# Fourier-convolution and gated-unit kernel: the loads of the second Fourier stage move from SyncE's queue to GpSimd's

## The chip, the cores and the metric

The kernel runs on one core of one Trainium2 chip. A core has five engines that run side by side: TensorE (PE in the profile; its weight loads are shown as PEld), VectorE (DVE), ScalarE (ACT), GpSimd (POOL) and SyncE (SP). An engine executes its own instructions in order; semaphores hold an instruction until what it needs from another engine has been done. DMAs between the chip's main memory (HBM, here also called DRAM) and the on-chip memory are issued from the queue of an engine and carried by 16 DMA engines. The metric is the device time of one execution in microseconds; the median of several runs is compared.

## The reference: what is computed

Two branches read the same input `x`, 2048 rows of 512 channels, and a sigmoid gate per row mixes them. Branch A is a long convolution per channel (a state-space layer): its kernel K of 2048 taps is a sum over 128 complex exponentials per channel, and the convolution is done by Fourier transforms of length 4096. Branch B is a bilinear gated unit with 1792 hidden channels.

```python
g = _sigmoid((x * gate_w).sum(-1, keepdims=True))
# branch A
P = jnp.exp((A * dt[:, None])[:, :, None] * pos[None, None, :])
K = 2.0 * jnp.einsum("dn,dnl->dl", C, P).real
Kf = jnp.fft.rfft(K, L2)
Uf = jnp.fft.rfft(u_t, L2)
y = jnp.fft.irfft(Uf * Kf[None, :, :], L2)[:, :, :L]
# branch B
h = jnp.einsum("bsd,df->bsf", x, w_gate) * jnp.einsum("bsd,df->bsf", x, w_up)
b = jnp.einsum("bsf,fd->bsd", h, w_down)
return g * a + (1 - g) * b            # a = y + u * D_skip
```

## The kernel before

**Branch B** is the bulk of TensorE's work. The hidden channels are cut into 14 tiles of 128 (index f), taken in four groups of three or four tiles; the 2048 rows are cut into four pieces of 512. Every fp32 product is made of three matmuls, since each operand is split into a high and a low part (`whi`/`wlo` for the first weights, `xs` for the input, `hh`/`hl` for the hidden values, `dhi`/`dlo` for the second weights). Matmuls into `pg` and `pu` are the two first products, matmuls into `y` the second. The `raw` tile (two buffers) receives weights before they are split. ScalarE evicts a `y` bank into an `acc` tile (three buffers), scaled by one minus the gate. In the first group `acc` is written to the output by SyncE; in the later groups `evacuate` has GpSimd issue a DMA that adds it to the output in memory (`out<-acc`).

**Branch A** works with matmuls of 32 or 64 partitions that go to the PSUM tile `k`. `u_part` does the first Fourier stage of the input and writes it to DRAM as `su_d`, with DMAs from GpSimd's queue. For each of 16 small blocks of 32 channels, VectorE and ScalarE make tables (`v`, `x`, `ri`, `su`, `t`) of powers, and `k_block` multiplies them on TensorE (`k<-v,x`). After every fourth block `k_first` does the first Fourier stage of the convolution kernel for 128 channels and writes it to DRAM as `sk_d`. Then `transforms(q)`, for q = 0 to 3 (128 channels each), does the rest. It takes four steps T: `m_load` brings a slice of both spectra from `su_d` and `sk_d`, with the two halves of the partitions in DMAs of their own, so four DMAs a step and 64 in all, each of 256 KB in rows of 128 floats; `m_second` is the second Fourier stage (`k<-in,w2s`, in the last block `k<-x,w2s` and `k<-v,w2s`), ScalarE or VectorE evicts it to `ev`; `m_product` multiplies the spectra on VectorE; every second step `m_inverse` goes back (`k<-y,w3s`) and its result `ts` is written to `y_d`. `m_last` reads `y_d`, finishes the inverse and adds to the output in memory from GpSimd's queue (`out<-ts`, `out<-in`, `out<-x`).

The loads of `m_load` go into the tile `in` for q below 3 (two buffers, shared with other loads), so the loads of step T + 2 wait for the matmuls of step T. For q = 3 they go into two `x` tiles and a `v` tile of the table pool and need not wait for one another. A load of `su_d` waits only for the writes of the input's stage; a load of `sk_d` waits until `k_first`'s writes for its q have landed.

**The order of the work** is fixed before the kernel is built, by a planner inside it (class `Work`). Each piece of work is added with an engine, an estimated duration, what it reads and writes, a rank and sometimes an earliest time. `Work.run` simulates all engines: it always takes the piece that can start first, on equal start the one of lower rank, books its duration, and for a DMA adds 1.3 us, its share of a common transfer rate, and 0.5 us. The pieces are then issued in that order, and `InOrder` ties each engine's instructions to it. So an estimate changes the order on all engines, not only on its own. Further rules of the planner: branch B's steps are paced by `T_STEP = 9.85`, and two groups of the small matmuls keep `APART = 6.0` us from one another (`LESS = 4.0` for the last q).

The functions that the change touches, with their callers:

Of the kernel before, what the change touches and what calls it, by code (L numbers as in the profile page):

```python
# [164 lines left out]
class Work:  # L165
# [27 lines left out]
    def add(self, engine, us, fn, r=(), w=(), rank=1, after=0.0, dma=0, hold=(), rows=(), many=0):  # L193


        task = Task(len(self.tasks), engine, us, fn, rank, after, dma)
        task.rows, task.many = rows, many
        self.tasks.append(task)
        clash = lambda p, q: p is None or q is None or p == q
        split = lambda x: x if isinstance(x, tuple) else (x, None)  # L200
        for tile, part in map(split, r):
            task.deps.update(t for p, t in tile.writers if clash(p, part))
        for tile, part in map(split, w):
            task.deps.update(t for p, t in tile.writers + tile.readers if clash(p, part))
        for tile, part in map(split, r):
            tile.readers.append((part, task))
        for tile, part in map(split, w):
            tile.writers.append((part, task))
        for tile, _ in map(split, [*r, *w, *hold]):
            if tile.pool and tile not in task.tiles:  # L210
                task.tiles.append(tile)
                tile.users.append(task)
        task.deps.discard(task)
        return task
# [105 lines left out]
def gated_mix_kernel(  # L320
# [16 lines left out]
    pe, dve, act, sp, pool_q = (InOrder(tc, e) for e in (nc.tensor, nc.vector, nc.scalar, nc.sync, nc.gpsimd))  # L337
# [22 lines left out]
    def new(pool, tag, shape, dtype=F32, bufs=1, loose=False):  # L360
        return work.tile(pools[pool], tag, shape, dtype, bufs, loose)
# [5 lines left out]
    def inp(shape):  # L367
        return new("mid", "in", shape, bufs=2)
# [718 lines left out]
    def m_load(q, T):  # L1087

        if q < KT - 1:
            t, at = inp([P, 8, 2, P]), lambda: t.t  # L1090
        elif T < 2:
            t = new("tab", "x", [P, 8, 2, P], bufs=2)
            at = lambda: t.t
        else:
            if T == 2:
                late["v"] = new("tab", "v", [P, 2, 8, 2, P])
            t = late["v"]
            at = lambda: t.t[:, T - 2]
        for w, (src, m) in enumerate(((su_d, m_su), (sk_d, m_sk))):
            for p in range(2):  # L1100
                r0 = 64 * p + 16 * T
                add(
                    "sp", 0.42,
                    lambda w=w, src=src, p=p, r0=r0: sp.dma_start(
                        at()[64 * p : 64 * p + 64, :, w], src[q, r0 : r0 + 16].rearrange("(j e) n d -> (e n) j d", e=2)
                    ),
                    r=[(m, (q, n0)) for n0 in range(0, 32, 8 if w else 4)], w=[(t, (T, w, p))], dma=256,
                )
        return at, [(t, (T, w, p)) for w in range(2) for p in range(2)]
# [184 lines left out]
    def transforms(q):  # L1294
# [4 lines left out]
        def loads(T):  # L1299
            return (  # L1300
                w_load("w2s", [P, 8, 32], w2[:, 8 * T : 8 * T + 8, :]),
                m_load(q, T),
                w_load("w3s", [P, 2, 2, 2, 64], w3[:, 2 * T : 2 * T + 2]),
            )
# [109 lines left out]
```

## Time and profile before

| | |
|---|---|
| median of 3 runs | 612.05 us (611.96 to 612.87) |
| the profiled execution: its time | 614.24 us |
| its span, first to last instruction | 612.5 us |
| granted TensorE clock, mean | 0.991 |
| TensorE busy | 587.5 us (96%) |
| VectorE busy | 526.5 us (86%) |
| ScalarE busy | 390.9 us (64%) |
| GpSimd busy | 68.2 us (11%) |
| SyncE's DMA queue (q1) | 105.00 MB, 59.6% of 16 DMA engines' span |
| GpSimd's DMA queue (q0) | 23.60 MB, 20.5% |

Times in the profile are microseconds unless marked as ns. A row of a table of instructions names the line of the code (here nearly always L119, that of the helper `InOrder`, so the tiles tell the operations apart), the engine, the operation, the written tile, an arrow and the read tiles; x4 means four instructions. A note such as "[3.32 <-issue]" or "<-DVE dlo" gives the idle time of the engine before the instruction and what ended it. SPq is SyncE's queue. Register, semaphore and DMA-issuing instructions aren't counted as busy, except GpSimd's, whose DMA instructions take its own time. A matmul's end is modelled, so busy TensorE is not TensorE at its peak.

### The profile page before, as it was taken

The numbers are of one execution on the slowest core, as the hardware profiler recorded it, in microseconds if no ns is written. First come the engines' busy times: TensorE is split into PE (matmuls) and PEld (weight loads), VectorE is DVE, ScalarE is ACT, GpSimd is POOL, SyncE is SP. The second block draws the span as 40 slices with busy tenths as digits, with TensorE's granted clock in tenths as the row PEclk, the third lists the DMA queues.
The fourth block names the chain that finished last, engine by engine and source line by source line (L and its number), as shares of the span: only waits on it lengthen the run. The fifth ranks groups of instructions, "written<-read, shape, count | busy, mean of one in ns | idle before, by whom it ended". The sixth has DMA issues, their size and how long they took to land.

```text
span 612.5 us, 15824 instructions
## 1 busy us (share of the span) xinstructions
PE 587.5 (96%) x6500; PEld 445.1 (73%) x6500; DVE 526.5 (86%) x841; ACT 390.9 (64%) x879; POOL 68.2 (11%) x109
## 2 busy tenths in 40 slices
PE   8889998999999999999999999997999999998993
PEld 5647676788877787787677878755788777775772
DVE  6999999999999999999799999978899943465625
ACT  5279688686678588758947766786666433433521
POOL 0011212100111020201211002002001002011101
PEclk9999999999999999999999999999999999998998
DMA  8999978676557996759989837879967279999756
GB/s 282 330 346 332 357 265 309 176 193 221 74 159 196 227 218 195 148 157 278 253 183 231 193 111 169 182 236 216 205 138 163 49 206 309 263 279 235 134 139 120
DMA packets 97948, 129.73 MB, mean 212 GB/s; under 512 B 6868, under 2 KB 68308, under 8 KB 95444
## 3 DMA queue, kind: packets, MB, share of 16 engines
q1 hardware_dynamic: 81268, 105.00, 59.6%
q0 software_dynamic: 16192, 23.60, 20.5%
q8 instruction: 51, 0.84, 0.6%
q14 instruction: 21, 0.17, 0.1%
q10 hardware_dynamic: 416, 0.13, 0.1%
HBM read 73.65 MB, written 55.05 MB: 210 GB/s over the span
## 4 chain that ended last, share of the span: by engine, by line
PE 72%; DVE 14%; issue 7%; ACT 4%; DMA 3%; POOLq 0%; SPq 0%; DVEq 0%; ACTq 0%; POOL 0%
PE pg L119 20%; PE pu L119 19%; PE y L119 19%; PE k L119 13%; DVE v L119 3%; DVE x L119 2%; DMA raw<-in_wts 2%; DVE y L119 1%; DVE h L119 1%; DVE ri L119 1%; DVE wlo L119 1%; ACT ts L119 1%; DVE t L119 1%; DMA y<-in_xT 1%; ACT acc L119 1%
## 5 line engine op out<-in xcount | busy, mean ns | idle before, releaser
L119 PE MATMUL pg<-xs,whi 128*128 128x512 f32 x448 | 139.9, 394 | 0.9 <-DVE xs L119 0.7
L119 PE MATMUL pu<-xs,whi 128*128 128x512 f32 x448 | 138.5, 390 | 0.0
L119 PEld LDWEIGHTS pg<-xs,whi 128*128 128x128 f32 x448 | 84.8, 190 | 20.9 <-ACT whi L119 1.8
L119 PEld LDWEIGHTS pu<-xs,whi 128*128 128x128 f32 x448 | 84.4, 188 | 17.2
L119 PE MATMUL y<-dhi,hl 128*128 128x512 f32 x224 | 90.9, 406 | 6.2 <-issue 3.3
L119 PE MATMUL pg<-xs,wlo 128*128 128x512 f32 x224 | 90.9, 406 | 3.3 <-ACT h L119 2.4
L119 PE MATMUL y<-dlo,hh 128*128 128x512 f32 x224 | 88.3, 394 | 1.9 <-DVE dlo L119 1.9
L119 PE MATMUL pu<-xs,wlo 128*128 128x512 f32 x224 | 89.2, 398 | 0.0
L119 PE MATMUL y<-dhi,hh 128*128 128x512 f32 x224 | 88.1, 394 | 0.0
L119 POOL DMA_DIRECT2D out<-acc x44 | 39.0, 939 | 350.1 <-ACT acc L119 303.9
L119 ACT CAST hh<-h 128x512 fp32r<-128x512 f32 x56 | 34.9, 622 | 60.1 <-DVE h L119 60.1
L119 ACT COPY ev<-k 128x512 f32<-128x512 f32 x112 | 59.6, 599 | 19.7 <-PE k L119 19.7
L119 ACT ACTIVATE acc<-y,ngate 128x512 f32<-128x512 f32 x63 | 42.7, 687 | 28.6 <-PE y L119 20.6
L119 PEld LDWEIGHTS y<-dhi,hl 128*128 128x128 f32 x224 | 42.4, 189 | 22.8 <-issue 5.1
L119 PEld LDWEIGHTS pg<-xs,wlo 128*128 128x128 f32 x224 | 42.4, 189 | 22.7 <-issue 6.5
L119 PEld LDWEIGHTS pu<-xs,wlo 128*128 128x128 f32 x224 | 42.1, 188 | 14.2 <-issue 5.4
L119 PEld LDWEIGHTS y<-dlo,hh 128*128 128x128 f32 x224 | 42.4, 189 | 13.7 <-issue 3.5
L119 ACT COPY h<-pg 128x512 f32<-128x512 f32 x56 | 33.1, 590 | 26.7 <-PE pg L119 20.6
L119 DVE TENSOR_TENSOR h<-pu,h 128x512 f32<-128x512 f32 x56 | 38.6, 689 | 12.8 <-PE pu L119 11.8
L119 PEld LDWEIGHTS y<-dhi,hh 128*128 128x128 f32 x224 | 42.6, 190 | 9.2
L119 DVE TENSOR_TENSOR hl<-h,hh 128x512 fp32r<-128x512 f32 x56 | 38.5, 688 | 4.3 <-ACT hh L119 4.3
L119 PEld LDWEIGHTS k<-v,x 128*32 128x32 f32 x2048 | 30.5, 109 | 5.9 <-issue 5.2
(118 smaller groups left out, 942.5 us busy)
## 6 DMA issues: line engine op xcount, KB each, us to landing
xs<-xs_d SPq DMA_DIRECT2D x36, 512.0 KB, 6.3
out<-acc POOLq DMA_DIRECT2D x44, 256.0 KB, 6.6
raw<-in_wts SPq DMA_DIRECT2D x36, 256.0 KB, 3.4
xs_d<-xs SPq DMA_DIRECT2D x16, 512.0 KB, 6.1
su_d<-ev POOLq DMA_DIRECT2D x32, 256.0 KB, 5.1
y_d<-ts SPq DMA_DIRECT2D x14, 512.0 KB, 5.2
in<-su_d SPq DMA_DIRECT2D x24, 256.0 KB, 7.3
sk_d<-ev SPq DMA_DIRECT2D x6, 1024.0 KB, 4.7
```

The source lines that it names most:

```text
L119: got = getattr(self.engine, name)(*args, **kw)
```

## The change

In `m_load` (line 1087) the 64 loads are issued by GpSimd (`pool_q`) instead of SyncE (`sp`), and the planner is told 1.2 us on GpSimd instead of 0.42 us on SyncE for each. What is loaded, from where, into which tile and after which writes stays as it is.

```diff
             for p in range(2):
                 r0 = 64 * p + 16 * T
                 add(
-                    "sp", 0.42,
-                    lambda w=w, src=src, p=p, r0=r0: sp.dma_start(
+                    "pool", 1.2,
+                    lambda w=w, src=src, p=p, r0=r0: pool_q.dma_start(
                         at()[64 * p : 64 * p + 64, :, w], src[q, r0 : r0 + 16].rearrange("(j e) n d -> (e n) j d", e=2)
                     ),
                     r=[(m, (q, n0)) for n0 in range(0, 32, 8 if w else 4)], w=[(t, (T, w, p))], dma=256,
```

## The prediction

> **What bounds the kernel now.** I read the page's totals first, then the busy time by stage, then the chain that ended last, then the queues that the change touches. First the page: the span, TensorE's line, and the chain's shares by engine.
>
> ```profile
> span 612.5 us, 15824 instructions
> PE 587.5 (96%) x6500; PEld 445.1 (73%) x6500; DVE 526.5 (86%) x841; ACT 390.9 (64%) x879; POOL 68.2 (11%) x109
> PE 72%; DVE 14%; issue 7%; ACT 4%; DMA 3%; POOLq 0%; SPq 0%; DVEq 0%; ACTq 0%; POOL 0%
> ```
>
> TensorE is busy for all but 25.0 us, and most of the chain is its matmuls; neither SyncE's queue nor GpSimd's holds a share. Now the stages: the columns are the stage, its length, then each engine's busy time.
>
> ```profile
> 0.00:120.00 120.00, 111.83 (x663) 80.32 (x664) 111.46 (x209) 83.74 (x182) 18.34 (x57) 1.00 0.85 301
> 120.00:390.00 270.00, 269.00 (x3461) 210.75 (x3460) 262.29 (x397) 198.39 (x463) 27.13 (x30) 1.00 0.77 187
> 390.00:450.00 60.00, 55.25 (x617) 39.18 (x616) 51.81 (x80) 44.98 (x110) 6.66 (x6) 0.97 0.98 217
> 450.00:540.00 90.00, 90.00 (x1054) 70.26 (x1054) 59.86 (x91) 39.40 (x77) 6.89 (x8) 1.00 0.76 191
> 540.00:570.00 30.00, 28.32 (x387) 19.86 (x369) 20.74 (x32) 12.16 (x27) 3.43 (x4) 0.94 0.96 237
> 570.00:612.50 42.50, 33.15 (x342) 24.77 (x341) 20.31 (x37) 12.23 (x25) 5.72 (x4) 0.95 0.66 133
> ```
>
> Idle TensorE time, length minus busy: 8.2 us before 120, 9.4 after 570, and between them 1.0 + 4.75 + 0 + 1.7 = 7.4 us. All of the moved loads but the first four are issued in that middle. So little can be won there (7.4 us and what follows the stalls), while a loss has no such limit. That asymmetry shapes the forecast.
>
> **The change, part by part.** The moved instructions are 64 DMAs: four Fourier blocks, four steps T each, two spectra, two halves of the partitions.
>
> *Removed from SyncE.* The price of one is the median of the middle figure (ns, minimum/median/maximum) below; the rows below it show GpSimd's nearest DMAs (busy us, mean ns).
>
> ```profile
> L119 SPq DMA_DIRECT2D in<-su_d x24: 579/634/3290, 116.0 to 442.7; - x24
> L119 POOL DMA_DIRECT2D out<-acc x44 | 39.0, 939 | 350.1 <-ACT acc L119 303.9 <-DMA w_t<-in_w 37.5 <-DVE t L119 5.2
> L119 POOL DMA_DIRECT2D su_d<-ev x32 | 17.4, 550 | 96.3 <-ACT ev L119 96.3
> L119 POOL DMA_DIRECT2D out<-ts x4 | 6.3, 1576 | 53.9 <-DVE ts L119 36.3 <-DMA out<-acc 9.8 <-DVE ri L119 6.2
> ```
>
> 64 x 0.634 = 41 us of issuing leave SyncE. Does anything of TensorE's wait behind it? The busiest place is the start of the third block, where the loads stand between weight loads (raw):
>
> ```profile
> 414.69 0.69 DVE L119 TENSOR_TENSOR wlo<-raw,whi 128x512 fp32r<-128x512 f32 x1
> 415.40 0.47 SPq L119 DMA_DIRECT2D raw<-in_wts  x1
> 415.92 3.87 SPq L119 DMA_DIRECT2D in<-sk_d  x4
> 419.36 0.71 DVE L119 TENSOR_TENSOR wlo<-raw,whi 128x512 fp32r<-128x512 f32 x1
> 420.10 10.23 SPq L119 DMA_DIRECT2D raw<-in_wts  x2
> ```
>
> Each raw load leaves within 0.03 us of the DVE instruction that frees its buffer (414.69 + 0.69 = 415.38; 419.36 + 0.71 = 420.07), so the loads ahead of it cost it nothing. I take the gain at 0. What hides the removed time is this wait for a buffer; its upper bound is the faster rival below.
>
> *Added to GpSimd.* No row shows such a load there. 256 KB written in larger pieces takes 0.55 us (su_d). 512 KB accumulated in 1024 pieces of 512 bytes takes 1.58 us, and 256 KB accumulated in 128 pieces (out<-acc) 0.94. A load has 512 pieces (64 partitions x 8 rows), so an estimate is 0.55 + 384/896 x (1.58 - 0.94) = 0.82 us, with 0.55 and 1.58 as ends. 64 x 0.82 = 52 us; GpSimd goes from 68 to about 121 us busy, no bound. The kernel's planner books 1.2 us instead of 0.42, so in its reckoning a step's four loads end 4 x 0.78 = 3.1 us later, the two that hold up a block's first step 1.6 us.
>
> *What lies on the path: the first step of a block.* Its kernel spectrum (sk_d) can only be loaded when it has been written back. Loads and the matmul group that they feed:
>
> ```profile
> 198.26 2.67 SPq L119 DMA_DIRECT2D in<-sk_d  x4
> 205.50 1.49 PE L119 MATMUL k<-in,w2s 32*32 32x256 f32 x64
> 213.27 1.49 PE L119 MATMUL k<-in,w2s 32*32 32x256 f32 x64
> 432.35 1.49 PE L119 MATMUL k<-in,w2s 32*32 32x256 f32 x64
> 522.87 3.59 SPq L119 DMA_DIRECT2D x<-sk_d  x4
> 538.76 1.49 PE L119 MATMUL k<-x,w2s 32*32 32x256 f32 x64
> in<-su_d SPq DMA_DIRECT2D x24, 256.0 KB, 7.3
> in<-sk_d SPq DMA_DIRECT2D x24, 256.0 KB, 7.5
> su_d<-ev POOLq DMA_DIRECT2D x32, 256.0 KB, 5.1
> out<-acc POOLq DMA_DIRECT2D x44, 256.0 KB, 6.6
> out<-ts POOLq DMA_DIRECT2D x4, 512.0 KB, 9.5
> ```
>
> By the median of 7.5 us the second load of the first block (198.26 + 0.63) lands at 206.4, though the group began at 205.50: no slack. The third block's (about 416.9) lands at 424.4, 8 us early; the fourth's (about 523.8) at 531, again 7 early. Later steps have more: the loads for 213.27 were out by 200.9. GpSimd's landings are 5.1 and 6.6 for this size and 9.5 for twice the size; the loads' small pieces put them between, so I keep 7.5 there, with 5.1 and 9.5 as ends. So the issue itself adds 2 x (0.82 - 0.63) = 0.4 us to one tight first step, and the planner, which fixes TensorE's order, books 1.6 for each of four. Ends: -2.4 us (landing at 5.1, one tight step) and +6.4 (all four). I take +1.5, one step put off in the order, since only one is tight; the cover otherwise is gated-unit matmuls, which can run at any time.
>
> *Queued on GpSimd with them.* Output accumulations (out<-acc) now share a queue in strict order with the loads. They come in fours and have three buffers:
>
> ```profile
> 214.36 0.85 POOL L119 DMA_DIRECT2D out<-acc  x1 [25.59 <-ACT acc L119]
> 215.26 1.35 SPq L119 DMA_DIRECT2D in<-su_d  x2
> ACT acc L119 <- DMA out<-acc: 6.3, 4, 3.5
> 514.43 0.69 ACT L119 ACTIVATE acc<-y,ngate 128x512 f32<-128x512 f32 x1 [3.45 <-DMA out<-acc]
> SPq L119 <- PE k L119: 111.0, 32, 13.3
> ```
>
> ScalarE already waits 6.3 us, four times, for an accumulation to land, at most 3.5. TensorE lost nothing at 514 (busy 90.00 of 90.00 us). Four loads ahead of a burst add 4 x 0.82 = 3.3 us of issue. Its cover is one gated-unit product, 24 matmuls, two of the 2.72 us rows quoted below: 5.4 us. So 3.5 + 3.3 = 6.8 exceeds it by 1.4 us where the two meet. Ends: 0 (never) and 11 x 1.4 = 15 us (in each of the 44/4 bursts). I take one meeting at this worst, rounded to +1.0, because only one of the four present waits is near its cover.
>
> *Sum:* 0 + 1.5 + 1.0 = +2.5 us. The profiled execution took 614.24 us for its 612.5 of span, 1.7 more; it stands 0.36% above the median of 612.05. The same difference on the median gives 614.5 us.
>
> By the Trainium skill (DMA: Bandwidth & Descriptors, "Issuing engines are not separate DMA queues") another issuing engine saves only sequencer time, as all DMAs share the same engines: by that rule the sum would be 0 and the time 612.0. No row here contradicts it; what it leaves out is the order within a queue.
>
> **The rivals.**
>
> *Faster: TensorE's two stalls go.* In the stages with a DMA share near 1 the tensor engine stalls for nothing the profile names, and then runs slowly:
>
> ```profile
> 427.23 0.51 PE L119 MATMUL y<-dhi,hl 128*128 128x512 f32 x1 [3.32 <-issue]
> 427.23 4.51 PE y L119 x12
> 557.54 1.69 issue
> 561.39 2.56 PE pg L119 x6
> 86.30 2.72 PE y L119 x12
> ```
>
> 3.32 + (4.51 - 2.72) + 1.69 + (2.56 - 1.36) = 8.0 us: 604.0 us if both vanish, 608 with the first alone, which I take. For it: the loads of 415.92 are issued and landing in the 11 us before the first stall, and another order may spread them. Against it: nothing ties the stalls to SyncE's queue. It decides once the order saves more than the 2.5 us above.
>
> *No change:* everything stays under matmuls, 612.0 us. For it: slack of 7 to 8 us in two blocks. Against it: the planner orders nearly 500 us of work anew.
>
> *Much slower: a load blocks GpSimd's queue.* SyncE waits 111 us, 32 times, up to 13.3, for matmuls to free load buffers. Where such a wait stands ahead of a burst, ScalarE's 3.5 grows to 16.8, 11.4 over the cover, with 1.8 of slow clock behind it: +13, 625 us; two waits of the mean 3.5 + 3.3 give 2 x (3.5 + 6.8 - 5.4 + 1.8) = +13 too. I take half, +8: 620 us. For it: loads and bursts meet at 214 to 215. Against it: GpSimd had been idle for 25.6 us before the burst at 214, so there is room between bursts. It decides when a wait at the queue's head passes 5.4 us.
>
> *Starved descriptors.* The row that bears on it is GpSimd beside a full VectorE:
>
> ```profile
> 60.00:90.00 30.00, 29.95 (x165) 21.79 (x163) 29.58 (x51) 22.55 (x46) 6.43 (x12) 1.00 0.84 307
> ```
>
> 12 DMAs took 6.43 us, 0.54 each, with VectorE 99% busy: no lock seen. If each load took 3 us instead, four would take 12 and the tight first steps would be late by 2 x 2.4 in four blocks, some 19 us: 631 us. The Trainium skill (SBUF — State Buffer, "SBUF: two separate sides") warns that VectorE's two-port modes lock GpSimd out while it writes descriptors, 620 ns becoming 3100; by that rule this rival holds, but the trace disagrees for the instructions run here.
>
> That the loads stay where they are cannot be: the call itself changes.
>
> **How the numbers follow.** Two measurements of this kernel differ by up to 0.15% (611.96 to 612.87), so 0.2%, 1.2 us, is about what can be told from no change. Small loss (613.3 to 618): 0.42. Faster: 0.30. No change: 0.13. Blocked queue: 0.12; starved: 0.03. Slower in all 0.57. The predicted 614.5 is the small loss's. The range, 605.0 to 622.0, takes in the faster rival to within 1 us of its full price and the middle of the blocked queue; I leave 0.05 below and 0.10 above. The small loss's own range is 613.3 to 618.
>
> **What would show it.** Right: in the changed profile the loads stand under GpSimd with 0.6 to 1.3 us each and GpSimd near 120 us busy; ScalarE's wait for out<-acc above 6.3 us; first steps at or after their old places; TensorE's idle between 120 and 570 near 10 us, not 7.4. Wrong: TensorE's idle there below 5 us with the stalls at 423 and 557 gone (faster), or an idle stretch beyond 5 us behind an accumulation that a load held up (much slower), or loads above 2 us (starved). What would upset the method is the planner's new order: a wholly different order near 390 to 570 could move the end by several microseconds for reasons that no row here prices.

## The result and the profile after

The changed kernel takes 608.69 us (median of seven runs, 606.53 to 609.36), the kernel before 612.18 us in the seven runs beside it (611.59 to 614.54). The ratio is 0.9929, with a 95% interval from 0.9907 to 0.9951. It is faster by 0.7%, where the forecast was a small loss; the time lies inside the forecast's range.

The page of the changed kernel: span, busy times, two DMA queues and the chain's shares.

```profile
span 606.9 us, 15872 instructions
PE 586.3 (97%) x6500; PEld 444.8 (73%) x6500; DVE 527.0 (87%) x841; ACT 389.8 (64%) x879; POOL 113.9 (19%) x173
q1 hardware_dynamic: 47476, 88.21, 45.8%
q0 software_dynamic: 21312, 40.38, 33.1%
PE 67%; DVE 16%; DMA 10%; issue 4%; ACT 2%; POOLq 0%; SPq 0%; ACTq 0%; DVEq 0%; POOL 0%
```

The same two queues on the page before (packets, MB, share of the 16 DMA engines):

```profile
q1 hardware_dynamic: 81268, 105.00, 59.6%
q0 software_dynamic: 16192, 23.60, 20.5%
```

The 16.8 MB of loads have changed queue, and GpSimd is busy for 113.9 us instead of 68.2. TensorE's busy time fell by 1.2 us and the span by 5.6. Where the rest went shows in the stages of the changed kernel, with the columns that the prediction named (length, then busy TensorE, its weight loads, VectorE, ScalarE, GpSimd, then granted clock, DMA share, GB/s).

```profile
0.00:120.00 120.00, 111.72 (x663) 80.83 (x664) 111.40 (x209) 83.72 (x182) 21.08 (x61) 0.99 0.84 300
120.00:390.00 270.00, 269.62 (x3460) 210.69 (x3459) 264.22 (x398) 197.04 (x459) 47.61 (x58) 1.00 0.76 187
390.00:450.00 60.00, 57.50 (x568) 41.80 (x569) 54.27 (x87) 46.41 (x118) 15.04 (x18) 0.97 0.92 203
450.00:540.00 90.00, 90.00 (x1111) 69.48 (x1111) 60.64 (x92) 39.25 (x76) 21.07 (x28) 1.00 0.76 199
540.00:570.00 30.00, 30.00 (x445) 21.46 (x443) 22.77 (x35) 13.03 (x28) 3.47 (x4) 1.00 0.89 242
570.00:606.90 36.90, 27.45 (x261) 20.57 (x259) 13.70 (x25) 10.39 (x23) 5.67 (x4) 0.91 0.77 156
```

TensorE's idle time between 120 and 570 us is 0.38 + 2.50 + 0 + 0 = 2.9 us, where it was 7.4. Both stalls of the kernel before, 3.32 us at 427 and 1.69 at 557, are gone. Before 120 the idle time is 8.3 (was 8.2), after 570 it is 9.45 (was 9.35). So the 5.6 us are 4.5 of idle time in the middle and 1.2 of busy time, less 0.2 at the ends, with rounding. The largest idle stretch that is left in the middle is a new one, at 432.

### The profile page after: what moved, and what is told of

Same layout as the page of the kernel before. It is cut to its first block, busy times and chain, and to the rows that moved or that the text cites. A ratio compares the mean times of both kernels' runs of the same rounds, so it can differ in the third digit from the quotient of the medians.

```text
span 606.9 us, 15872 instructions
## 1 busy us (share of the span) xinstructions
PE 586.3 (97%) x6500; PEld 444.8 (73%) x6500; DVE 527.0 (87%) x841; ACT 389.8 (64%) x879; POOL 113.9 (19%) x173
## 3 DMA queue, kind: packets, MB, share of 16 engines
q1 hardware_dynamic: 47476, 88.21, 45.8%
q0 software_dynamic: 21312, 40.38, 33.1%
## 4 chain that ended last, share of the span: by engine, by line
PE 67%; DVE 16%; DMA 10%; issue 4%; ACT 2%; POOLq 0%; SPq 0%; ACTq 0%; DVEq 0%; POOL 0%
PE pg L119 19%; PE pu L119 18%; PE y L119 17%; PE k L119 13%; DMA raw<-in_wts 5%; DVE v L119 3%; DVE x L119 2%; DMA y_d<-e 2%; DMA dt_d<-small 2%; DVE wlo L119 1%; DVE y L119 1%; DVE ri L119 1%; DVE t L119 1%; DVE m L119 1%; DMA x<-dt_d 1%
## 5 line engine op out<-in xcount | busy, mean ns | idle before, releaser
L119 POOL DMA_DIRECT2D su_d<-ev x32 | 17.4, 550 | 96.4 <-ACT ev L119 96.4
```

The lines of the kernel that those rows point to most:

```text
L119: got = getattr(self.engine, name)(*args, **kw)
```

## The experiments

The change does two things at once. It moves 64 loads to another queue, and, because the planner is told another engine and another duration, it reorders all engines' work. The **queue theory** says that the time changed because the loads left SyncE's queue. The **order theory** says that it changed because the work was planned anew. The first three experiments separate the two; in each of them the order of TensorE's, VectorE's and ScalarE's instructions is that of the kernel before or of the changed one exactly. The diffs below are cut to the changed lines and at most two around them. They are against the kernel before, but for the last one.

**The changed kernel once more.**

> The changed kernel once more, so that it shares a chip and its runs of the kernel before with the next three. Both theories: ratio to before 0.993 (0.991 to 0.995), some 608 to 609 us.

It took 608.32 us (605.62 to 609.03), ratio 0.9931 (0.9908 to 0.9953). The gain repeats.

**The queue alone**: the planner is told what it was told before, and only the issuing engine changes.

```diff
                 add(
                     "sp", 0.42,
-                    lambda w=w, src=src, p=p, r0=r0: sp.dma_start(
+                    lambda w=w, src=src, p=p, r0=r0: pool_q.dma_start(
```

> Only the queue is moved: the planner is told 0.42 us on SyncE as before, so TensorE, VectorE and ScalarE keep the old order instruction by instruction, and the 64 loads are issued by GpSimd. Theory queue (SyncE relieved, or the loads travelling in another ring, makes the gain): ratio 0.993, about 608.5 us, and the 3.3 us idle of TensorE at 427 and the 1.7 at 559 gone. Theory order (the planner's new order makes the gain, the queue nothing): ratio 1.000, 612 us, TensorE idle between 120 and 570 still near 7.4 us.

It took 613.89 us (612.66 to 614.89) against 612.58 for the kernel before in the same series: ratio 1.0029 (1.0013 to 1.0045). Moving the loads costs a little. The stage from 390 to 450 us, and TensorE's row in it:

```profile
390.00:450.00 60.00, 54.12 (x488) 37.82 (x487) 49.65 (x75) 42.78 (x95) 16.60 (x22) 0.94 0.94 210
```

```profile
428.80 0.80 PE L119 MATMUL y<-dhi,hl 128*128 128x512 f32 x1 [3.77 <-ACT x L119]
```

The first stall is still there, 3.77 us before the same matmul, and TensorE is idle for 5.9 us of this stage (4.75 in the kernel before). So the queue theory doesn't explain the gain.

**The order alone**: the planner is told the new values, and SyncE issues the loads.

```diff
                 add(
-                    "sp", 0.42,
+                    "pool", 1.2,
                     lambda w=w, src=src, p=p, r0=r0: sp.dma_start(
```

> Only the order is moved: the planner is told 1.2 us on GpSimd, so TensorE, VectorE and ScalarE have the changed kernel's order instruction by instruction, but SyncE issues the 64 loads. Theory order: ratio 0.993, about 608.5 us, idle between 120 and 570 near 2.9 us. Theory queue: ratio 1.000 or a little above, 612 to 613 us.

It took 605.42 us (604.73 to 606.12), ratio 0.9890 (0.9871 to 0.9908). This is below both kernels; its interval and that of the changed kernel meet only at their ends. Its stages, in the same columns:

```profile
120.00:390.00 270.00, 269.14 (x3455) 210.23 (x3455) 263.73 (x397) 196.90 (x457) 27.16 (x30) 1.00 0.78 186
390.00:450.00 60.00, 58.87 (x601) 43.73 (x591) 57.65 (x91) 48.34 (x122) 6.54 (x6) 1.00 0.95 205
540.00:570.00 30.00, 30.00 (x507) 22.04 (x506) 20.52 (x32) 14.65 (x34) 5.21 (x6) 1.00 0.93 244
```

Idle time in the middle is 0.86 + 1.13 + 0 = 2.0 us. In this order the whole gain comes from the planner, 7.2 us by the medians, and the queue gives 2.9 of it back (608.32 less 605.42). In the old order the queue costs 1.3 us (613.89 less 612.58). Two questions remain: what the stalls are, and where the queue's cost lies.

**A third planner's value, with the loads on GpSimd.**

```diff
                 add(
-                    "sp", 0.42,
-                    lambda w=w, src=src, p=p, r0=r0: sp.dma_start(
+                    "pool", 0.75,
+                    lambda w=w, src=src, p=p, r0=r0: pool_q.dma_start(
```

> Loads on GpSimd, and the planner told 0.75 us, the price that the changed kernel's profile shows for one (0.72 median). This gives a third order of TensorE's work. Theory queue: as fast as the changed kernel, ratio 0.993, since it has the same queue. Theory order: any value between 0.990 and 1.005, since a new order is a new draw; a ratio near 1.000 would speak for it.

It took 613.74 us (611.11 to 615.19), ratio 1.0019 (1.0004 to 1.0035), and both stalls are in its trace (3.56 us before 429.61, 0.95 before 563.21). The first of them:

```profile
429.61 0.79 PE L119 MATMUL y<-dhi,hl 128*128 128x512 f32 x1 [3.56 <-ACT x L119]
```

A truer estimate of GpSimd's price (it measured 0.72) gives a worse order than the 1.2 of the change.

**What the stalls are.** In the kernel before, the eight loads of the third block's first two steps are issued between 412 and 420 us, the four of the convolution kernel's spectrum from 415.92 on. The DMA queue's rows for the stretch from 416 to 420 us, then those for the half microsecond from 424 to 424.5 (packets, MB, share of 16 engines in the stretch; the packets' times add up, so it can pass 100%):

```profile
q1 hardware_dynamic: 1391, 0.79, 119.3%
```

```profile
q8 instruction: 1, 0.02, 17.3%
```

The second queue is the one that fetches instructions. Over the execution it has 51 packets of 16,384 bytes; TensorE's records (13,000 matmuls and weight loads, 119 of its sequencer) number 13,119, which is 257 for each packet. I counted in the trace how many TensorE instructions had begun by the start and by the end of each fetch, less 256 for each earlier fetch. At the end of the fetch at 424.24 this count is 449, and it was 449 at its start too: TensorE began nothing while the fetch was under way, and nothing until 427.23. At the end of the fetch at 556.74, where the second stall stands, it is 449 again.

So I formed a third theory: the fetch of TensorE's next instructions is delayed behind the loads' packets, and TensorE runs dry. (With the loads on GpSimd's queue the profile names ScalarE's copy `x` as what ended the first stall. In the kernel before, that copy ended at 424.90, and TensorE stood until 427.23 all the same.) The theory predicts that the stall goes if the loads do, with TensorE's order untouched. In the next kernel the loads of the third block's first two steps are replaced by a fill on GpSimd, in the old order.

```diff
-                    lambda w=w, src=src, p=p, r0=r0: sp.dma_start(
+                    (lambda w=w, p=p: pool_q.memset(at()[64 * p : 64 * p + 64, :, w], 0.0))
+                    if q == 2 and T < 2
+                    else lambda w=w, src=src, p=p, r0=r0: sp.dma_start(
```

> The kernel before with its order on TensorE, VectorE and ScalarE, SyncE's queue for the loads, but the eight loads of the first two steps of the third block (2 MB, issued 412 to 420 us) are left out; GpSimd sets their tiles to zero instead, so the third block's convolution is wrong. Theory fetch (TensorE's stall at 427 is a 16 KB fetch of its own instructions that comes late because the DMA engines are full): the fetch of 424 comes several microseconds earlier and the stall is below 0.5 us; with its slow clock 3.3 + 1.8 = 5 us go, ratio about 0.992. Theory wait (TensorE waits there for ScalarE, as the profile of the old order with GpSimd's queue names it): the stall stays at 3 us or more, ratio 0.998 to 1.000.

It took 608.07 us (606.61 to 610.56), ratio 0.9918 (0.9888 to 0.9948). Its DMA rows from 416 to 420 us, its stage, and TensorE's row that answers to the one after the stall:

```profile
q1 hardware_dynamic: 144, 0.26, 24.8%
q8 instruction: 1, 0.02, 1.4%
```

```profile
390.00:450.00 60.00, 58.29 (x639) 42.36 (x639) 56.30 (x90) 48.49 (x119) 14.27 (x14) 1.00 0.84 186
```

```profile
423.51 0.39 PE L119 MATMUL y<-dhi,hl 128*128 128x512 f32 x1
```

Without those 2 MB the fetch comes at 419.70, 4.5 us earlier, with the count at 316 at its start, and TensorE runs through. The granted clock of the stage is 1.00 where it was 0.97. The later loads are as they were, and there a stall remains: 1.14 us before 553.33, with the count at 445.

Two more planner's values test whether the stalls go where the fetches go, and whether the gain grows with the value.

```diff
-                    "sp", 0.42,
+                    "sp", 0.63,
```

> The kernel before with only the planner's price of a load on SyncE changed, 0.42 to 0.63 us, what the profile of before shows. Theory draw (the gain is the luck of one order): a third order, anything from 0.988 to 1.005. Theory direction (dearer loads make a better order): a part of the gain, ratio 0.994 to 0.998. If the order hardly differs where the stalls are, both give 1.000 and it tells nothing.

```diff
-                    "sp", 0.42,
+                    "pool", 1.6,
```

> Loads issued by SyncE, the planner told 1.6 us on GpSimd instead of 1.2. Theory direction: at least as fast as with 1.2, ratio 0.989 or below, 605 us or less. Theory draw: anything from 0.985 to 1.010; a ratio above 0.995 would speak for it.

In both, SyncE issues the loads. The first took 610.46 us (608.50 to 612.18), ratio 0.9949 (0.9929 to 0.9970), the second 612.57 (609.74 to 614.85), ratio 0.9989 (0.9969 to 1.0010); the kernel before took 613.43 beside them. The second one's row for TensorE, and the fetch that ends in that stall, from the DMA rows from 551.5 to 552 us:

```profile
554.70 0.69 PE L119 MATMUL k<-y,w3s 32*64 32x128 f32 x31 [2.74 <-issue]
```

```profile
q8 instruction: 1, 0.02, 18.5%
```

The first kernel keeps both stalls, shorter (2.09 us before 425.76, 1.02 before 557.09); its time fits both of the theories named for it. The second refutes the idea that a dearer load makes a better order: at 1.6 the gain is all but gone. Its stalls stand at other places (219.53 and 554.70), and the count at them is the same. Over ten profiled executions (the kernel before, the changed kernel twice, and the seven others of this section) there are 510 such fetches; at the end of none of them is the count above 449. It is 449 where TensorE stood longest: 3.32 and 1.69 us in the kernel before, 3.77 and 1.56 with the queue alone, 3.56 at the value of 0.75, 2.09 at 0.63, 1.55 and 2.74 at 1.6. In the changed kernel and in the order alone the highest is 438 to 439, and no idle stretch of TensorE between 120 and 570 us that is put down to issue is longer than 0.31 us. In all eight stalls at 449 the next matmul begins 1.3 to 1.7 us after the fetch has ended, whether the stall lasted 1.55 us or 3.77. And one count at all of them means that TensorE stopped each time at the same place in its blocks of 256.

What the new order changes in the trace is when the burst comes. In the changed kernel the block's first load leaves at 421.65, when the fetch of this stretch has ended (418.04); the next fetch runs from 425.38 to 426.74, and the count at its end is only 226. In the order alone the first load leaves at 424.16, and the fetch ahead of it has ended at 420.20.

That the loads make the first stall is shown, by taking them out. That the fetch is what stands between them is supported by the count, which no order exceeded, and by the restart just after the fetch, but no run changed the fetch alone; that this fetch queue is TensorE's I infer from the number of packets. The Trainium skill (Runtime: NRT & Kernel Launch, "Instruction fetch mechanics") says that a sequencer fetches blocks of 16 KiB, 256 instructions, by a DMA queue of its own while it executes the present block, and that this is mostly hidden. The block and the ratio agree with the trace; that it is hidden doesn't hold where the DMA engines are full, as 3.32 us with no instruction begun show.

**Where the queue's cost lies.** In the changed kernel the idle time before 432.68 is the largest in the middle. GpSimd's rows, SyncE's row, the chain's rows, and ScalarE's row there:

```profile
421.65 1.61 POOL L119 DMA_DIRECT2D in<-su_d  x2
423.10 0.84 POOL L119 DMA_DIRECT2D in<-sk_d  x1
```

```profile
415.56 12.68 SPq L119 DMA_DIRECT2D raw<-in_wts  x3
```

```profile
424.70 6.80 DMA raw<-in_wts
432.68 4.59 PE pg L119 x12
```

```profile
431.52 0.62 ACT L119 CAST dhi<-raw 128x512 fp32r<-128x512 f32 x1 [0.65 <-DMA raw<-in_wts]
```

```profile
432.68 0.50 PE L119 MATMUL pg<-xs,wlo 128*128 128x512 f32 x1 [2.02 <-ACT h L119]
```

SyncE's row holds three weight loads with no load of a spectrum between them, and the second of them leaves at 424.70, when its buffer comes free. By then GpSimd has issued three loads of the block. That weight load takes 6.8 us to land; ScalarE waits for it, its copy of `h` comes late, TensorE is idle for 2.02 us and then runs 12 matmuls in 4.59 us. On SyncE's queue, in the same order, the weight load stands ahead of those loads, as the rows of the order alone show:

```profile
414.57 9.48 SPq L119 DMA_DIRECT2D raw<-in_wts  x2
424.16 1.71 SPq L119 DMA_DIRECT2D in<-su_d  x2
```

Standing behind the loads has the same price on either queue: in the kernel before, the weight load of 415.40 left behind four loads on SyncE's own queue and took 6.8 us as well (the row is of the window from 412 to 416 us; the load of 407.59, ahead of the burst, took 2.5).

```profile
raw<-in_wts SPq DMA_DIRECT2D x1, 256.0 KB, 6.8
```

The next kernel gives only the third block's loads back to SyncE; its diff is against the changed kernel.

```diff
-                    lambda w=w, src=src, p=p, r0=r0: pool_q.dma_start(
+                    lambda w=w, src=src, p=p, r0=r0: (sp if q == 2 else pool_q).dma_start(
```

> The changed kernel, its order and GpSimd's queue, except that the 16 loads of the third block (q = 2) are issued by SyncE. Theory local (GpSimd's queue costs its 3 us where those loads meet the weight loads, at 424 to 433): the stall at 432 falls from 2.0 to 2.7 us to about 1.1 and the ratio to before to 0.989, 605.5 us, as with all loads on SyncE. Theory spread (the cost comes from accumulations held up behind loads at every burst): at most a quarter of it goes, ratio 0.992, 607.5 us.

It took 606.02 us (604.00 to 606.63), ratio 0.9876 (0.9854 to 0.9897). SyncE's rows for the weight load and the loads, the chain's row, and the stage:

```profile
415.53 9.48 SPq L119 DMA_DIRECT2D raw<-in_wts  x2
425.06 1.91 SPq L119 DMA_DIRECT2D in<-su_d  x2
```

```profile
431.89 3.02 PE pg L119 x12
```

```profile
390.00:450.00 60.00, 58.89 (x631) 43.41 (x620) 57.02 (x91) 48.22 (x123) 6.46 (x6) 1.00 0.93 204
```

The weight load leaves at 424.7 as in the changed kernel, now ahead of the loads, and lands in 2.7 us. The same 12 matmuls take 3.02 us, the idle time before them is 1.11, the clock of the stage is 1.00. That is 0.91 + 1.57 = 2.5 us at this one place, close to the 2.9 us that the queue costs in this order. The interval meets that of the order alone (0.9871 to 0.9908), so the other 48 loads cost nothing measurable on GpSimd's queue.

In the old order the same thing shows in the trace of the queue alone, though no run tested it. GpSimd issues the third block's first loads from 410.36 on, and a weight load that leaves SyncE's queue at 411.83 takes 8.9 us to land; in the kernel before it left at 411.56, ahead of them, and took 4.0. ScalarE now waits for it, where it did not wait before, and TensorE waits for ScalarE:

```profile
420.76 0.62 ACT L119 CAST whi<-raw 128x512 fp32r<-128x512 f32 x1 [2.62 <-DMA raw<-in_wts]
422.02 0.50 PE L119 MATMUL y<-dhi,hl 128*128 128x512 f32 x1 [0.79 <-ACT acc L119]
```

These 0.79 us and the 0.45 by which the first stall is longer account for the 1.1 us by which the stage's idle time grew, and that is most of the queue's 1.3.

## Why the prediction was right or wrong

**Removed from SyncE, taken at 0: right.** With TensorE's order fixed, taking the loads off SyncE gained nothing in either order. The cover named for it, the wait for a free weight buffer, is still there. The reason was half the story: the weight loads left on time, but behind the loads they landed late (6.8 us for that of 415.40), and the forecast looked only at when they left.

**Added to GpSimd, 0.82 us a load: right, a little high.** GpSimd's loads (ns, minimum/median/maximum), their landing, and ScalarE's wait for accumulations (us, times, longest) in the changed kernel:

```profile
L119 POOL DMA_DIRECT2D in<-su_d x24: 686/720/1367, 116.9 to 457.3; - x24
L119 POOL DMA_DIRECT2D in<-sk_d x24: 686/714/1192, 197.8 to 458.6; - x24
in<-su_d POOLq DMA_DIRECT2D x24, 256.0 KB, 7.9
ACT acc L119 <- DMA out<-acc: 3.3, 1, 3.3
```

The price is 0.72 us, GpSimd's total 113.9 where about 121 was forecast, and the landing 7.9 where 7.5 was kept. The starved rival is refuted: the longest load took 1.37 us, though VectorE was busy for 264.22 of the 270 us from 120 to 390.

**The first step of a block, +1.5: this step failed.** It read the planner's new estimate as a delay only. The delay is there, but TensorE doesn't pay for it. In the changed kernel the third block's first step stands here:

```profile
L119 PE MATMUL k<-in,w2s x64: 374/374/398, 438.6 to 439.7; 32*32 32x256 f32 x64
```

That is 6.2 us later than the 432.35 of before (438.56 less 432.35), in a stage where TensorE's idle time fell by 2.25 us: other matmuls took the place. The tight step of the first block, at 205.5, didn't move at all. The other effect of a new estimate, that the work of all engines is ordered anew, I had named as what would upset the method and had given no size in the sum. Alone it measured -7.2 us, and what it moved, the burst of loads against TensorE's instruction fetches, no term of the sum had in it.

**Output accumulations behind the loads, +1.0: wrong mechanism.** ScalarE's wait for them was to rise above 6.3 us; it fell to 3.3. In the kernel with the third block's loads back on SyncE it did rise, to 7.2, and that kernel is the faster of the two (ratio 0.9876 against 0.9931). The queue does cost, 1.3 us in the old order and 2.9 in the new one, so the sign and the size of the term came out about right by luck. In the new order the cause is a weight load on SyncE that the moved loads overtake. The prediction had asked what the loads delay on the queue they go to, and not what they had been waiting behind on the queue they left.

**The sum.** The queue's terms, 0 + 1.0, stand against 1.3 to 2.9 measured; the order's term, +1.5, against -7.2. The Trainium skill's rule that another issuing engine saves only sequencer time (DMA: Bandwidth & Descriptors, "Issuing engines are not separate DMA queues") would have the queue alone change next to nothing; it measured +0.29%, with an interval that leaves out zero.

**The faster rival, 0.30: this is what happened.** It priced both stalls at 8.0 us with the slow clock behind them, which gives 604.0. Both went, and the order alone stands at 605.4; the queue's loss brings it to 608.3. The 608 given for the first stall alone agrees by accident, and it doesn't follow from the rival's own figures: 3.32 + 1.79 = 5.1 us leave 606.9. The run without the loads, in which the first stall alone went, was 5.4 us faster (608.07 against 613.43). "Nothing ties the stalls to SyncE's queue" was true and beside the point: the first is tied to the loads, on either queue. The rival's sentence that another order may spread the loads came near the mechanism. The fetch at 424.24 was in the trace of before; reading the stall's DMA rows would have tied the stall to the burst and raised this chance. It wouldn't have made it certain, since an order at 0.75 kept both stalls and one at 1.6 made new ones.

**Blocked queue, no change: neither.** The blocked queue's condition was met: loads at the head of GpSimd's queue waited for matmuls far longer than 5.4 us, the longest time here:

```profile
283.33 1.46 POOL L119 DMA_DIRECT2D in<-su_d  x2 [30.00 <-PE k L119]
```

Its consequence, an idle stretch of TensorE beyond 5 us, didn't follow; between 120 and 570 us none is longer than 2.02, and ScalarE's longest wait for an accumulation is 3.3. No change fell to what the prediction had set against it, the new order of the work.

## What to carry to other kernels

Where a planner fixes the order, a changed estimate is a change of its own: take the edit apart into the queue and the order before explaining either, since here they had opposite signs and the order alone (605.4 us) is faster than both together (608.3). A stall for "issue" in a stage where the DMA engines are full is worth a look at the instruction fetches in that stretch; here thinning the burst in front of the fetch removed it, and so did an order that brings the burst later. Loads on a queue of their own no longer wait their turn behind the loads that matter more; here it paid to keep on the critical loads' queue those few that would overtake them.

## What the hardware showed that was not expected

A burst of loads stopped TensorE, by all signs through its instruction supply. With SyncE's packets at 119.3% of the engines' time, the fetch came at 424.24 rather than 419.70, and TensorE stood for 3.32 us at 449 counted instructions, the ceiling that no fetch in any of the profiles passed.

The gain from an order isn't monotone in the estimate that makes it. With the loads on SyncE and the planner told 0.63 us on SyncE, 1.2 on GpSimd or 1.6 on GpSimd, the ratios were 0.995, 0.989 and 0.999; with the loads on GpSimd, told 0.75 or 1.2 on GpSimd, they were 1.002 and 0.993.

The same load makes other packets on another queue. SyncE's queue lost 81,268 - 47,476 = 33,792 packets, 528 for each of 64 loads of 256 KB; GpSimd's gained 21,312 - 16,192 = 5,120, or 80 each, so 3.2 KB a packet instead of 0.5. The share of the DMA engines' time went from 80.1% for the two queues to 78.9% of a shorter span. So fewer, larger packets hardly saved transfer time here. In the one order the landing of the `su_d` loads was 7.9 us on GpSimd's queue and 8.3 on SyncE's.
